# A gated linear attention block followed by a leaky-ReLU MLP on one core: units 0 to 3 as batches of 256 tokens, weights behind unit 0's v, DMA transposes in units 6 to 11, fixed tiles and banks, a new order

## The chip, the cores and the metric

The kernel runs on one core of a Trainium2 chip. The core has five engines, each with a queue of its own that it works through in order: TensorE (PE; PEld is its weight load), VectorE (DVE), ScalarE (ACT), GpSimd (POOL) and SyncE (SP, which here only issues DMAs). Sixteen DMA engines move data between the chip's memory and the core. The metric is the time of one execution in device microseconds.

## The reference

Four batches, eight heads, 768 tokens, 48 columns a head. The first part is a recurrence with a decay per key column; its output, 384 columns a token, goes through a two-layer MLP of width 2048.

```python
f = 1.0 / (1.0 + np.exp(-f_logit))
state = np.zeros((B, H, D, D), dtype=np.float32)
for t in range(S):
    state = f[:, :, t, :, None] * state + np.einsum('bhd,bhe->bhde', k[:, :, t], v[:, :, t])
    y[:, :, t] = np.einsum('bhd,bhde->bhe', q[:, :, t], state)
x = y.transpose(0, 2, 1, 3).reshape(B * S, H * D)
h = x @ w_in
out = np.maximum(0.01 * h, h) @ w_out
```

Inputs and output are float32; the kernel's matmuls are bf16 into float32.

## The kernel before

The recurrence is done in chunks of 128 tokens. With cumulative sums of the log decays, k is scaled up and q scaled down, so that inside a chunk the result is a masked product (q k^T) v, and what came before is q times a state matrix that is carried from chunk to chunk and decayed at its end.

A *unit* is one chunk of two batches: unit j is chunk j // 2 of batches 2(j % 2) and 2(j % 2) + 1, twelve units in all. 128 tokens lie on the 128 partitions, one token to a partition, and the two batches side by side. For a unit, the parts run in this sequence (in brackets the word that stands for each in the order list):

- loads of f, k, q, v by SyncE (`Lf`, `Lk`, `Lq`, `Lv`, line 98), one DMA for each batch of the unit: 128 partitions times 8 heads, 192 bytes a piece. Six buffers for each of the four inputs.
- ScalarE: Exp and Ln of the gate (`gate`, lines 121 and 122).
- TensorE: cumulative sum over tokens as a product with a triangular matrix, and sums over the whole chunk (`cs`, lines 127 and 130).
- ScalarE: three Exp of these (`dec`, lines 137 to 141).
- VectorE or GpSimd: k and q times their factors (`k`, `q`, lines 146 and 152); GpSimd: casts of v (`v`, lines 159 and 160). A cast `v_b` and a zero-padded copy `v2` serve the product with v in strips of 32 columns.
- TensorE: transposes of k and q through an identity matrix, four to a group (`tk`, `tq`, line 173); VectorE copies them out of PSUM (`ck`, `cq`, line 176).
- TensorE: products of k and q (`sc`, called score, line 192); VectorE: the mask (`mk`, line 197).
- TensorE: products with v and with the state (`mx`, mix, line 225); VectorE copies the result out as `xT` (`xt`, line 231).
- state: TensorE (`pt`, line 236), VectorE adds it (`sf`, lines 241 and 242), GpSimd decays and casts it (`sb`, lines 246 and 249).
- MLP: eight `up` (line 256, six matmuls of 256 columns each, a pair of 128-wide blocks of the hidden layer), eight relus on ScalarE (`pr`, line 262), for each of the two batches four quarters of `down` (`dn`, line 267, four matmuls of 384 columns each), VectorE's copy (`ob`, line 272) and the store by SyncE (`st`, line 277).

The weights are loaded by GpSimd with a cast to bf16 (`WI`, line 107, nine DMAs; `WO`, line 111, four). Ahead of each stands a one-element copy (line 103) that waits for the v of a unit: unit 1 for w_in, unit 2 for w_out.

Nothing reorders the work: a list of words in the kernel gives the order in which all instructions are issued, and each engine's queue is this list cut down to its own. The engines run apart from each other as far as data and buffers allow. PSUM has three pools: two banks for `up`, two for `down`, four for everything else.

Of the kernel before, what the change touches and what calls it, by code (L numbers as in the profile page):

```python
# [9 lines left out]
FP32 = mybir.dt.float32  # L10
BF16 = mybir.dt.bfloat16
# [4 lines left out]
def kernel(  # L16
# [21 lines left out]
    pairs = [(c, h) for c in range(NCH) for h in range(B // 2)]  # L38
    NP = len(pairs)
    BY_UNIT = 4  # L40
    K_DVE = 3
    Q_DVE = 2

    const = ctx.enter_context(tc.tile_pool(name="const", bufs=1))
    inp = ctx.enter_context(tc.tile_pool(name="inp", bufs=6))
    work = ctx.enter_context(tc.tile_pool(name="work", bufs=2))
    gpool = ctx.enter_context(tc.tile_pool(name="gpool", bufs=4))
    opool = ctx.enter_context(tc.tile_pool(name="opool", bufs=4))

# [19 lines left out]
    ut = const.tile([128, 128], BF16, tag="ut")  # L69
    make_upper_triangular(nc, ut, val=1.0, diag=True)  # L70
# [3 lines left out]
    nc.gpsimd.memset(ones_col, 1.0)  # L74
    gate_w = const.tile([1, 8], FP32, tag="gate_w")

    w_in_b = const.tile([128, NK, FF], BF16, tag="w_in")
    w_out_b = const.tile([128, NF, KD], BF16, tag="w_out")

    for t in v2s:  # L80
        nc.gpsimd.memset(t[:, :, 1:3, :], 0.0)
    for t in state_b + state_f:
        nc.gpsimd.memset(t, 0.0)

    st = {j: {} for j in range(NP)}
    srcs = {"f": f_logit, "k": k, "q": q, "v": v}

    def once(j, key, make):
        if key not in st[j]:
            st[j][key] = make()  # L90
        return st[j][key]

    def raw(j, name):
        return once(j, name + "_raw", lambda: inp.tile([128, 2, H, D], FP32, name=f"{name}_raw", tag=f"{name}_raw"))

    def load(j, name, a):
        c, h = pairs[j]
        nc.sync.dma_start(out=raw(j, name)[:, a],  # L98
                          in_=srcs[name][2 * h + a, :, c * C:(c + 1) * C, :].rearrange("h t d -> t h d"))

    def weights(which, j):

        nc.gpsimd.tensor_copy(out=gate_w[:, 0:1], in_=raw(j, "v")[0:1, 1, H - 1, D - 1:D])
        if which == "in":
            for lo, hi in ((0, FF // 4), (FF // 4, FF // 2), (FF // 2, FF)):
                for kk in range(NK):
                    nc.gpsimd.dma_start(out=w_in_b[:, kk, lo:hi], in_=moe_w_in[kk * 128:(kk + 1) * 128, lo:hi])
        else:
            n = NF // 4
            for part in range(4):  # L110
                nc.gpsimd.dma_start(  # L111
                    out=w_out_b[:, part * n:(part + 1) * n, :],
                    in_=moe_w_out[part * n * 128:(part + 1) * n * 128, :].rearrange("(a p) n -> p a n", p=128))

    def half(j, i):
        return slice(i, i + 1) if j < BY_UNIT else slice(0, 2)

    def gate(j, i):
        e = work.tile([128, 2, H, D], FP32, name="e_t", tag="e_t")
        a = half(j, i)  # L120
        nc.scalar.activation(e[:, a], raw(j, "f")[:, a], AF.Exp, scale=-1.0)  # L121
        nc.scalar.activation(lfs[j % NR][:, a, :, 0:D], e[:, a], AF.Ln, bias=1.0)  # L122

    def cs(j, a):
        lf = lfs[j % NR]
        t = st[j]["cs", a] = ps_g.tile([128, 512], FP32, name="cs", tag="g")
        nc.tensor.matmul(t[:, 0:H * D], ut, lf[:, a, :, 0:D], start=True, stop=True)  # L127
        if pairs[j][0] < NCH - 1:
            for p in range(P2):
                nc.tensor.matmul(t[:, H * D + p:H * D + p + 1], lf[:, a, 2 * p:2 * p + 2, :], ones_col,  # L130
                                 start=True, stop=True)

    def dec(j, a):
        t = st[j].pop(("cs", a))
        em = once(j, "em", lambda: work.tile([128, 2, H * D], BF16, name="em_t", tag="em_t"))
        at = once(j, "a", lambda: work.tile([128, 2, H * D], BF16, name="a_t", tag="a_t"))
        nc.scalar.activation(em[:, a], t[:, 0:H * D], AF.Exp, scale=1.0)  # L137
        nc.scalar.activation(at[:, a], t[:, 0:H * D], AF.Exp, scale=-1.0)  # L138
        if pairs[j][0] < NCH - 1:
            end = st[j]["end", a] = work.tile([128, P2], FP32, name="a_end", tag="a_end", bufs=8)  # L140
            nc.scalar.activation(end, t[:, H * D:H * D + P2], AF.Exp, scale=-1.0)  # L141

    def scale_k(j, i):
        a = half(j, i)
        eng = nc.vector if j < K_DVE else nc.gpsimd
        eng.tensor_mul(khs[j % NR][:, a, :, 0:D], raw(j, "k")[:, a],  # L146
                       st[j]["em"][:, a].rearrange("t a (h d) -> t a h d", d=D))

    def scale_q(j, i):
        a = half(j, i)  # L150
        eng = nc.vector if j < Q_DVE else nc.gpsimd
        eng.tensor_mul(qhs[j % NR][:, a, :, 0:D], raw(j, "q")[:, a],  # L152
                       st[j]["a"][:, a].rearrange("t a (h d) -> t a h d", d=D))

    def cast_v(j, i):
        a = half(j, i)
        vb = once(j, "v", lambda: work.tile([128, 2, H, D], BF16, name="v_b", tag="v_b", bufs=3))
        v2 = once(j, "v2", lambda: v2s[j % 3])
        nc.gpsimd.tensor_copy(out=vb[:, a], in_=raw(j, "v")[:, a])  # L159
# [21 lines left out]
    def units(a):  # L181
        return range(2) if a == 2 else (a,)
# [199 lines left out]
```

## Time and profile before

| | us |
|---|---|
| median of three runs | 197.61 |
| lowest and highest of them | 197.46, 198.98 |
| span of the profiled execution | 195.7 |
| TensorE busy in the span | 177.3 |
| ScalarE, VectorE, GpSimd busy | 98.4, 93.4, 83.3 |

The profile shows one execution; its own time outside the span is not listed. The span runs from the first to the last instruction. In the profile's rows L256 is line 256 of the kernel; "po<-w_out_b,gT" names what is written and what is read; "SPq" and "POOLq" are the queues' issuing of DMAs. A busy TensorE is not TensorE at its peak, because the ends of matmuls are modelled and overlap.

### The profile page before, as it was taken

The numbers are of one execution on the slowest core, as the hardware profiler recorded it, in microseconds if no ns is written. First come the engines' busy times: TensorE is split into PE (matmuls) and PEld (weight loads), VectorE is DVE, ScalarE is ACT, GpSimd is POOL, SyncE is SP. The second block draws the span as 40 slices with busy tenths as digits, with TensorE's granted clock in tenths as the row PEclk, the third lists the DMA queues.
The fourth block names the chain that finished last, engine by engine and source line by source line (L and its number), as shares of the span: only waits on it lengthen the run. The fifth ranks groups of instructions, "written<-read, shape, count | busy, mean of one in ns | idle before, by whom it ended". The sixth has DMA issues, their size and how long they took to land.

```text
span 195.7 us, 5241 instructions
## 1 busy us (share of the span) xinstructions
PE 177.3 (91%) x2152; PEld 130.7 (67%) x2152; DVE 93.4 (48%) x203; ACT 98.4 (50%) x197; POOL 83.3 (43%) x145
## 2 busy tenths in 40 slices
PE   0686379999999999999979999999999999999993
PEld 0455237777667687787756867777777777777761
DVE  2699614273327438347581149168373146553111
ACT  5645415893234748776155752854324736154430
POOL 8145845928400762795332902984204420500000
PEclk9999999999999999999996999999999999999999
DMA  6999999899999999899999999220001110110112
GB/s 134 216 216 185 166 196 208 162 183 186 190 222 215 222 198 226 159 228 219 200 201 232 183 232 209 44 78 6 18 27 40 45 40 3 40 40 3 40 44 80
DMA packets 106728, 27.08 MB, mean 138 GB/s; under 512 B 100432, under 2 KB 106320, under 8 KB 106704
## 3 DMA queue, kind: packets, MB, share of 16 engines
q1 hardware_dynamic: 103296, 23.60, 57.1%
q0 software_dynamic: 3408, 3.15, 10.1%
q8 instruction: 17, 0.28, 0.6%
q14 instruction: 7, 0.06, 0.1%
HBM read 25.17 MB, written 4.72 MB: 153 GB/s over the span
## 4 chain that ended last, share of the span: by engine, by line
PE 69%; DMA 15%; SPq 11%; POOL 2%; issue 1%; ACT 1%; DVE 1%; POOLq 0%
PE po L267 30%; PE pm L256 25%; SPq L98 10%; DMA q_raw<-in_q_dram 7%; DMA w_out_b<-in_moe_w_out_dram 7%; PE py L225 4%; PE tp L173 4%; PE pw L192 2%; DMA f_raw<-in_f_logit_dram 1%; PE cs L127 1%; POOL w_out_b L111 1%; PE pt L236 1%; SPq L277 1%; POOL qh L152 0%; ACT e_t L121 0%
## 5 line engine op out<-in xcount | busy, mean ns | idle before, releaser
L262 ACT ACTIVATE gT<-pm 128x512 bf16<-128x512 f32 x96 | 57.0, 598 | 75.0 <-PE pm L256 74.5
L256 PE MATMUL pm<-xT,w_in_b 128*128 128x256 bf16 x576 | 79.7, 278 | 5.0 <-DMA w_in_b<-in_moe_w_in_dram 3.6
L267 PE MATMUL po<-w_out_b,gT 128*128 128x384 bf16 x384 | 75.9, 328 | 0.1
L256 PEld LDWEIGHTS <-w_in_b 128*128 128x128 bf16 x576 | 54.8, 99 | 19.1 <-DMA w_in_b<-in_moe_w_in_dram 4.4
L267 PEld LDWEIGHTS <-gT 128*128 128x128 bf16 x384 | 36.2, 98 | 17.2 <-issue 0.6
L197 DVE TENSOR_TENSOR wm<-pw,ut 128x512 bf16<-128x512 f32 x48 | 30.1, 683 | 9.1 <-PE pw L192 9.1
L272 DVE COPY osb<-po 128x384 f32<-128x384 f32 x24 | 13.4, 557 | 40.7 <-PE po L267 40.5
L246 POOL TENSOR_TENSOR sf<-sf,a_end 128x192 f32<-128x192 f32 x20 | 10.7, 535 | 27.1 <-DVE sf L242 26.4
L146 POOL TENSOR_TENSOR kh<-k_raw,em_t 128x768 bf16<-128x768 f32 (+1 forms) x10 | 15.0, 1495 | 15.0 <-ACT em_t L137 8.3
L249 POOL CAST sb<-sf 64x192 bf16<-64x192 f32 x40 | 14.2, 356 | 16.1 <-PE py L225 13.8
L159 POOL CAST v_b<-v_raw 128x384 bf16<-128x384 f32 (+1 forms) x16 | 10.9, 681 | 23.7 <-DMA v_raw<-in_v_dram 15.7
L231 DVE CAST xT<-py 128x384 bf16<-128x384 f32 x24 | 12.4, 553 | 15.7 <-PE py L225 15.2
L176 DVE COPY kT<-tp 128x512 bf16<-128x512 bf16 x24 | 9.8, 420 | 20.7 <-PE tp L173 20.7
L152 POOL TENSOR_TENSOR qh<-q_raw,a_t 128x768 bf16<-128x768 f32 (+1 forms) x12 | 16.8, 1399 | 0.5 <-DMA q_raw<-in_q_dram 0.4
L121 ACT ACTIVATE e_t<-f_raw 128x384 f32<-128x384 f32 (+1 forms) x16 | 11.0, 687 | 9.4 <-DMA f_raw<-in_f_logit_dram 9.3
L127 PE MATMUL cs<-lf,ut 128*128 128x384 bf16 x24 | 8.3, 366 | 7.3 <-ACT lf L122 6.6
L137 ACT ACTIVATE em_t<-cs 128x384 bf16<-128x384 f32 x24 | 11.8, 493 | 4.9 <-PE cs L130 4.6
L176 DVE COPY qT<-tp 128x512 bf16<-128x512 bf16 x24 | 9.8, 419 | 5.2 <-PE tp L173 5.0
L138 ACT ACTIVATE a_t<-cs 128x384 bf16<-128x384 f32 x24 | 12.0, 499 | 0.0
L122 ACT ACTIVATE lf<-e_t 128x384 bf16<-128x384 f32 (+1 forms) x16 | 10.9, 683 | 0.5
L173 PE MATMUL tp<-ident,kh 128*128 128x128 bf16 x96 | 9.6, 233 | 1.5 <-ACT a_end L141 1.0
L130 PEld LDWEIGHTS <-lf 128*128 128x128 bf16 x80 | 5.2, 103 | 8.1 <-issue 6.7
(40 smaller groups left out, 139.0 us busy)
## 6 DMA issues: line engine op xcount, KB each, us to landing
f_raw<-in_f_logit_dram SPq DMA_DIRECT2D x24, 192.0 KB, 3.7
k_raw<-in_k_dram SPq DMA_DIRECT2D x24, 192.0 KB, 3.7
q_raw<-in_q_dram SPq DMA_DIRECT2D x24, 192.0 KB, 3.8
v_raw<-in_v_dram SPq DMA_DIRECT2D x24, 192.0 KB, 3.8
out_dram<-osb SPq DMA_DIRECT2D x24, 192.0 KB, 2.0
w_out_b<-in_moe_w_out_dram POOLq DMA_DIRECT2D x4, 384.0 KB, 9.5
w_in_b<-in_moe_w_in_dram POOLq DMA_DIRECT2D x6, 128.0 KB, 6.1
w_in_b<-in_moe_w_in_dram POOLq DMA_DIRECT2D x3, 256.0 KB, 9.2
```

The lines of the kernel that those rows point to most:

```text
L98: nc.sync.dma_start(out=raw(j, name)[:, a], in_=srcs[name][2 * h + a, :, c * C:(c + 1) * C, :].rearrange("h t d -> t h d"))
L146: eng.tensor_mul(khs[j % NR][:, a, :, 0:D], raw(j, "k")[:, a], st[j]["em"][:, a].rearrange("t a (h d) -> t a h d", d=D))
L152: eng.tensor_mul(qhs[j % NR][:, a, :, 0:D], raw(j, "q")[:, a], st[j]["a"][:, a].rearrange("t a (h d) -> t a h d", d=D))
L173: nc.tensor.transpose(tp[:, p, :], scaled(j, x)[:, a, 2 * p:2 * p + 2, :], ident)
L176: nc.vector.tensor_copy(out=turned(j, x)[:, P2 * a:P2 * a + P2, :], in_=st[j].pop(("tp" + x, a)))
L197: nc.vector.tensor_mul(wm, st[j].pop(("pw", a, i)), ut[:, None, :].to_broadcast([128, P2, 128]))
L231: nc.vector.tensor_copy(out=xT[:, :, a, :], in_=st[j].pop(("py", a))[:, 0:NK, :])
L249: nc.gpsimd.tensor_copy(out=sb[rows, a, :, i * D:i * D + D], in_=sf[rows, a])
L256: nc.tensor.matmul(pm[:, i, :], w_in_b[:, kk, ff * 128:(ff + 1) * 128], st[j]["xT"][:, kk].rearrange("t a s -> t (a s)"), start=(kk == 0), ...
L262: nc.scalar.activation(gT[:, 2 * g:2 * g + 2, :], st[j].pop(("pm", g)), AF.Prelu, alpha=0.01)
L267: nc.tensor.matmul(po, st[j]["g"][:, ff, 128 * a:128 * a + 128], w_out_b[:, ff, :], start=(ff == 0), stop=(ff == NF - 1))
L272: nc.vector.tensor_copy(out=osb, in_=st[j].pop(("po", a)))
```

## The change

- **Units 0 to 3** are now batches: unit j holds chunks 0 and 1, that is 256 tokens, of batch j. Two neighbouring tokens lie on one partition, so a piece of a load has 384 bytes, and one DMA (`_2`) brings both halves of the heads; unit 0 is loaded in two halves of four heads. Chunk 0 lies on partitions 0 to 63 and chunk 1 on 64 to 127. The cumulative sum takes four matmuls of 192 columns with two triangular matrices (`bu`, `bs`, with and without the diagonal), the score takes 32 matmuls with 64 rows and 64 columns of the array each, the mix 64 matmuls with 64 rows and 32 columns, and the state part of chunk 1 follows in a step of its own (`ms`). These units are called *paired*.
- **Units 4 to 11** stay as they were: chunks 2 to 5 of two batches.
- **Weights.** The copy that holds w_in back reads unit 0's v (`Hv_0`), the one for w_out unit 2's k (`Hk_2`). w_in comes in three DMAs, w_out in four whose pieces are 6 KB long: partition p of a quarter holds rows 4p to 4p + 3. So that the hidden layer fits this, the weight loads of `up` read every fourth column of w_in.
- **Transposes** of units 6 to 11 are DMA transposes issued by SyncE (`xk`, `xq`) in place of TensorE's transposes and VectorE's copies. In units 0 and 1 six copies go to ScalarE.
- **Buffers.** All tiles are fixed and indexed by the unit's number; PSUM is eight banks, and each word in the list names its banks. `gT` has three buffers instead of four.
- **Set-up** on GpSimd: the masks `bu`, `bs`, `pair_mask`, `half_ones`, and eight `sb` tiles to clear instead of two `sb` and two `sf`.
- **Order.** A new list.

```diff
-    pairs = [(c, h) for c in range(NCH) for h in range(B // 2)]
+    NA = 4
+    units = [(b, None) for b in range(B)] + [(c, h) for c in range(2, NCH) for h in range(B // 2)]
...
+    PIECES = (512, 512, 1024)
+    w_in_b = [const.tile([128, NK, n], BF16, name=f"w_in{i}", tag=f"w_in{i}") for i, n in enumerate(PIECES)]
+    w_out_b = tiles(4, [128, 4, KD], BF16, "w_out")
+
+    def w_in_of(ff, kk):
+        g, jj = divmod(ff, 4)
+        lo = 512 * g
+        for t, n in zip(w_in_b, PIECES):
+            if lo < n:
+                return t[:, kk, lo + jj:lo + 512:4]
+            lo -= n
...
+            if paired(j):
+                h = slice(0, H) if a == 2 else slice(4 * a, 4 * a + 4)
+                nc.sync.dma_start(out=by_pair(raw(j, x))[:, h].rearrange("t h s d -> t h (s d)"),
+                                  in_=srcs[x][j, h, 0:2 * C, :].rearrange("h (t s) d -> t h (s d)", s=2))
...
+    def hold(x):
+        def go(j):
+            nc.gpsimd.tensor_copy(out=gate_w[:, 0:1], in_=raw(j, x)[0:1, 1, H - 1, D - 1:D])
+        return go
+
+    def load_w_in(i):
+        lo = sum(PIECES[:i])
+        nc.gpsimd.dma_start(out=w_in_b[i],
+                            in_=moe_w_in[:, lo:lo + PIECES[i]].rearrange("(k p) n -> p k n", p=128))
+
+    def load_w_out(g):
+        nc.gpsimd.dma_start(out=w_out_b[g],
+                            in_=moe_w_out[512 * g:512 * g + 512, :].rearrange("(p a) n -> p a n", a=4))
...
+        if paired(j):
+            h = slice(4 * a, 4 * a + 4)
+            for s in range(2):
+                o = t[:, 192 * s:192 * s + 192]
+                nc.tensor.matmul(o, bu, lf[:, 0, h, 0:D], start=True, stop=False)
+                nc.tensor.matmul(o, bu if s else bs, lf[:, 1, h, 0:D], start=False, stop=True)
+            for n in range(2):
+                p = 2 * a + n
+                for s in range(2):
+                    nc.tensor.matmul(t[:, 384 + 2 * n:386 + 2 * n], lf[:, s, 2 * p:2 * p + 2, :], half_ones,
+                                     start=(s == 0), stop=(s == 1))
+            return
...
+    def turn_dma(x):
+        def go(j):
+            nc.sync.dma_start_transpose(out=turned(j, x), in_=scaled(j, x).rearrange("t a h d -> t (a h d)"))
+        return go
...
+        if paired(j):
+            q2 = qT.rearrange("t (s p) n -> t p s n", s=2)
+            for s in range(2):
+                for n in range(2):
+                    p = 2 * a + n
+                    for i in range(2):
+                        for y in range(2):
+                            rows, cols = slice(64 * y, 64 * y + D), slice(64 * i, 64 * i + 64)
+                            o = banks[bank[y]][cols].rearrange("t (s p m n) -> t s p m n", s=2, p=2, m=2)
+                            nc.tensor.matmul(o[:, s, n], kT[rows, P2 * s + p, cols], q2[rows, p, :, cols],
+                                             start=True, stop=True)
+            return
...
+    def mix_state(j):
+        q2 = turned(j, "q").rearrange("t (s p) n -> t p s n", s=2)
+        jobs = []
+        for g in range(NQ):
+            p, n = divmod(g, 3)
+            jobs.append((1, g, state_of(j, 1)[:, p, 32 * n:32 * n + 32], q2[:, p, :, 64:128]))
+        accumulate(j, jobs, (1,))
...
+            if paired(j):
+                src = src.rearrange("t (k s n) -> t k s n", k=NK, s=2)
+                dst = xT[:, :, i, :].rearrange("t k (n s) -> t k s n", s=2)
```

The beginning of the new list, to the first `down`, and two later stretches of which the prediction speaks. A number behind @ is a bank; a last digit 1 in `k`, `q` stands for GpSimd, in `ck`, `cq` for ScalarE.

```
Lf_0_0 Lf_0_1 Lk_0_0 Lq_0_0 Lv_0_0 ge_0_0 Lk_0_1 gl_0_0 Lq_0_1 ge_0_1 cs_0_0@0 Lv_0_1 gl_0_1 Lf_1_2 cs_0_1@1
dec_0_0 Lk_1_2 k_0_0_0 v_0_0 Lq_1_2 dec_0_1 q_0_0_0 tk_0_0@2 Lv_1_2 k_0_1_0 tq_0_0@3 ck_0_0_1 Lf_2_2 q_0_1_0
tk_0_1@4 cq_0_0_1 Lk_2_2 tq_0_1@5 Hv_0 ck_0_1_1 v_0_1 sc_0_0@6.7 Lq_2_2 cq_0_1_1 Lv_2_2 WI_0 mk_0_0_0
pt_0_2@0.1 ge_1_0 Lf_3_2 mk_0_0_1 ge_1_1 sc_0_1@2.3 WI_1 gl_1_0 sf_0_0 mx_0_0@4.5 gl_1_1 Lk_3_2 mk_0_1_0
WI_2 cs_1_0@6 mk_0_1_1 sb_0_0 cs_1_1@7 dec_1_0 sf_0_1 Lq_3_2 mx_0_1 dec_1_1 q_1_0_1 k_1_0_0 k_1_1_0 ms_0
q_1_1_1 tk_1_0@0 xt_0_0_0 tq_1_0@2 ck_1_0_1 tk_1_1@3 xt_0_1_0 sb_0_1 tq_1_1@6 ck_1_1_1 cq_1_0_0 up_0_0@1
cq_1_1_0 up_0_1@7 pr_0_0 sc_1_1@4.0 pr_0_1 sc_1_0@5.2 mk_1_1_0 mk_1_0_0 up_0_2@3 mk_1_0_1 up_0_3@6 mk_1_1_1
pr_0_2 pr_0_3 Lv_3_2 v_1_0 up_0_4@1 v_1_1 up_0_6@7 Lf_4_0 ge_2_0 pr_0_4 pt_1_2@4.5 pr_0_6 up_0_5@2 sf_1_0
gl_2_0 Lk_4_0 Hk_2 WO_0 ge_2_1 mx_1_2@0.3 pr_0_5 sb_1_0 up_0_7@6 xt_1_0_0 gl_2_1 Lq_4_0 WO_1 sf_1_1 ms_1
pr_0_7 cs_2_0@1 WO_2 xt_1_1_0 cs_2_1@7 dec_2_0 Lv_4_0 sb_1_1 up_1_1@4 k_2_0_0 dec_2_1 up_1_5@2 k_2_1_0 WO_3
tk_2_0@0 pr_1_1 up_1_6@5 v_2_0 ck_2_0_0 pr_1_5 tk_2_1@6 pr_1_6 up_1_2@3 q_2_0_1 ck_2_1_0 dn_0_0_0@1 pr_1_2
...
dec_7_1 up_5_7@2 Lq_10_0 ob_4_0_0 ge_9_2 up_5_0@5 q_7_2_1 st_4_0 pr_5_7 up_5_4@6 pr_5_0 up_5_3@4 gl_9_2
...
pr_8_2 up_8_4@1 pr_8_0 up_8_3@4 pr_8_4 dn_8_0_0@0 pr_8_3 cs_11_0@6 cs_10_0@3 dn_8_1_0@2 dec_11_0 k_11_2_1
mx_9_2@5.7 dec_10_0 dn_8_1_1 xt_9_0_0 q_11_2_1 xt_9_1_0 xk_11 dn_8_0_1 up_9_4@1 up_9_3@4 q_10_2_1 pr_9_4
xq_11 dn_8_1_2 pr_9_3 up_9_6@6 k_10_2_1 xq_10 dn_8_1_3 pr_9_6 up_9_7@3 ob_8_1_0 dn_8_0_2 st_8_1 pr_9_7 xk_10
up_9_5@5 up_9_1@7 pr_9_5 up_9_2@1 pr_9_1 up_9_0@4 pr_9_2 dn_8_0_3 pr_9_0 sc_11_2@6.2.3.5 ob_8_0_0 dn_9_0_0@7
mk_11_0_0 st_8_0 dn_9_1_0@1 mk_11_1_1 dn_9_0_1 mk_11_0_1 mk_11_1_0 sc_10_2@4.0.6.5 dn_9_0_2 mk_10_0_0
```

572 lines of the change are left out of this document (342 added, 230 removed).

## The prediction

> **What bounds the kernel now.** I read the page first, then the chain of waits, then the timeline of the first 53 us.
>
> ```profile
> PE 177.3 (91%) x2152; PEld 130.7 (67%) x2152; DVE 93.4 (48%) x203; ACT 98.4 (50%) x197; POOL 83.3 (43%) x145
> ...
> PE   0686379999999999999979999999999999999993
> ...
> DMA  6999999899999999899999999220001110110112
> ```
>
> TensorE is full from about slice 7 on, with one dip in slice 21. The DMA engines are full from the start to slice 25 (about 125 us). So there are two limits side by side: the matmul stream, and the loads that feed it. The chain of waits (start, length, what) gives the prices:
>
> ```profile
> 7.33 0.68 SPq L98
> ...
> 21.10 0.70 SPq L98
> ...
> 38.38 12.87 DMA w_out_b<-in_moe_w_out_dram
> ...
> 52.97 5.20 PE po L267 x32
> ...
> 61.57 0.55 PE pw L192 x16
> 62.13 0.76 PE pm L256 x6
> 62.89 0.65 PE po L267 x4
> ...
> 65.36 0.90 PE py L225 x56
> ...
> 72.03 0.66 PE pm L256 x6
> ...
> 97.84 2.78 DMA f_raw<-in_f_logit_dram
> 100.65 0.85 ACT e_t L121
> ...
> 102.90 1.23 PE pm L256 x6
> ...
> 138.62 0.89 PE tp L173 x16
> ...
> 192.32 0.56 DVE osb L272
> ```
>
> In the full stretch one `up` (6 matmuls) costs 0.655, one quarter of `down` 0.65, a `score` 0.55 and 0.10 more in the group behind it (0.76 against 0.66), a `mix` 0.90 and the same 0.10, four transposes 0.222. The timeline gives a `cs` (0.27, from 42.88 to 43.15) and a `state` (0.17, to 43.32):
>
> ```profile
> 42.88 0.33 PE L127 MATMUL cs<-lf,ut 128*128 128x384 bf16 x1
> ...
> 43.15 0.33 PE L236 MATMUL pt<-v_b,kh 128*128 128x96 bf16 x4
> ...
> 43.32 0.81 PE L267 MATMUL po<-w_out_b,gT 128*128 128x384 bf16 x4
> ```
>
> Counting the order list at these prices: 96 `up` 62.9, 96 quarters 62.4, `score` 7.8 (ten full, four half), `mix` 11.1 (ten at 1.0, four first-chunk halves at 0.275), 48 transpose groups 10.7, `cs` 20 x 0.27 + 4 x 0.17 = 6.1, `state` 20 x 0.17 = 3.4. Sum 164.4. The last matmul ended at 192.3, when the final copy began, so **27.9 us of TensorE time were lost**. The list ahead of the row at 52.97 (20 `up`, 8 quarters, 4 half and 1 full `score`, the same of `mix`, 14 transpose groups, 8 `cs`, 6 `state`) is worth 28.6, so 24.4 of the 27.9 were lost before 53 us, and 3.5 after. Nearly all of the 3.5 is one event: the second half of unit 9's f is issued at 97.84, ScalarE stands at its Exp until 100.65, the relus behind it are late, and TensorE goes on at 102.90 with a slow group. Behind the last matmul the span has 3.4 us, and the median of the runs is 1.9 above the span of 195.7; the profiled execution's own time is not listed apart, so I carry this 1.9 as what lies around a span.
>
> **The change: the matmul stream.** `up` and `down` keep their counts: 125.3. Units 6 to 11 lose 24 transpose groups (DMA does them): -5.3. Paired units: each `cs` half has four 192-column and four 2-column matmuls instead of one 384-column and four: 0.27 + 0.17 = 0.44 by the columns streamed (384 take 0.163 in `down`), 8 of them. Their `score` has 32 matmuls of 64 rows and columns a unit; the nearest rows are 34 ns (0.55/16) and 16 ns (0.90/56) each, 0.51 to 1.10, I take 0.84. `mix` 64 matmuls of 64 rows, 8 to 16 ns, plus 12 for the state: 1.2 a unit (0.8 to 1.3). `state` 16 matmuls, 0.34 to 0.68, take 0.5. Sum: 125.3 + score 8.6 + mix 12.9 + transposes 5.3 + cs 7.4 + state 4.0 = **163.5** (160 to 167): the stream itself hardly changes.
>
> **The strided weights.** Each of the 576 `up` weight loads now reads every fourth column. No weight load before does.
>
> ```profile
> L256 PEld LDWEIGHTS <-w_in_b 128*128 128x128 bf16 x576 | 54.8, 99 | 19.1 <-DMA w_in_b<-in_moe_w_in_dram 4.4 <-issue 2.2
> ```
>
> The 99 ns is a latency: transposes follow each other at 0.89/16 = 55.6 ns, a load each. An `up` matmul takes 109 ns and covers the load. Twice 55.6 is 111: +2 ns x 576 = 1.1 us; four times is 222: +113 x 576 = 65 us. A gain is excluded, since the load is covered already. I take 0, as the cover is twofold. The Trainium skill (TensorE: Matmul & The Clock Gate, "Weight-path perf modes") says that fast weight load reads 32 bits, two bf16, at a time; with every fourth column that would halve the rate and the sum would be 1.1 us longer. No run here shows it.
>
> **Loads.** The nearest rows for the price of a piece are the loads' queue, a stretch in which only stores run, and the issues with their time to landing:
>
> ```profile
> q1 hardware_dynamic: 103296, 23.60, 57.1%
> ```
>
> ```profile
> 140.00:150.00 10.00, 10.00 (x143) 7.45 (x142) 6.23 (x13) 3.58 (x6) 1.67 (x4) 1.00 0.12 41
> ```
>
> ```profile
> v_raw<-in_v_dram SPq DMA_DIRECT2D x24, 192.0 KB, 3.8
> out_dram<-osb SPq DMA_DIRECT2D x24, 192.0 KB, 2.0
> ...
> w_out_b<-in_moe_w_out_dram POOLq DMA_DIRECT2D x4, 384.0 KB, 9.5
> ...
> w_in_b<-in_moe_w_in_dram POOLq DMA_DIRECT2D x3, 256.0 KB, 9.2
> ```
>
> From 140 to 150 us only stores run: share 0.12 of 16 engines, 410 KB, 267 rows of 1536 B, so 72 ns a row. The queue's 57.1% is 1788 us of engine time; less 3072 stored rows at 72 ns, 98,304 pieces of 192 B cost 15.9 ns each. A line through both gives 23.9 ns for the 384 B pieces of units 0 to 3 (bounds: 15.9, no cost by size; 31.8, no gain). 32,768 pieces become 16,384: 521 us become 392, and 129/16 = **8.1 us of DMA time go** (0 to 16.3), all in the first third.
>
> **The start.** Before the change w_in waits for unit 1's v and w_out for unit 2's (timeline; behind it rows of the groups):
>
> ```profile
> 19.20 0.18 POOL L103 COPY gate_w<-v_raw 1x1 f32<-1x1 f32 x1 [1.73 <-DMA v_raw<-in_v_dram]
> ...
> 24.77 0.53 POOL L107 DMA_DIRECT2D w_in_b<-in_moe_w_in_dram  x1 [0.98 <-DMA w_in_b<-in_moe_w_in_dram]
> 25.27 3.80 SPq L98 DMA_DIRECT2D v_raw<-in_v_dram  x1
> ...
> 26.46 1.03 PE L256 MATMUL pm<-xT,w_in_b 128*128 128x256 bf16 x4 [0.68 <-DMA w_in_b<-in_moe_w_in_dram]
> ...
> 29.12 5.05 SPq L98 DMA_DIRECT2D f_raw<-in_f_logit_dram  x1
> ...
> 35.98 0.18 POOL L103 COPY gate_w<-v_raw 1x1 f32<-1x1 f32 x1
> ```
>
> ```profile
> L176 DVE COPY kT<-tp 128x512 bf16<-128x512 bf16 x24 | 9.8, 420 | 20.7 <-PE tp L173 20.7
> ...
> L152 POOL TENSOR_TENSOR qh<-q_raw,a_t 128x768 bf16<-128x768 f32 x8 | 13.1, 1642 | 0.0
> ...
> L159 POOL CAST v_b<-v_raw 128x384 bf16<-128x384 f32 x8 | 4.3, 538 | 7.0 <-DMA v_raw<-in_v_dram 4.0 <-ACT a_t L138 3.0
> ...
> L83 POOL MEMSET sb<- 128x768 bf16 x2 | 1.4, 740 | 0.0
> L81 POOL MEMSET v<- 128x256 bf16 x3 | 0.8, 311 | 0.0
> ```
>
> After the change unit 0's v is the gate, the eighth load: issued by 8.0 with the old pieces, landed 3.8 later at 11.8, about 9.5 with the new ones. But GpSimd has its own list first: eight `sb` memsets of half the size (0.37 each, 3.0), 25 small set-up operations (0.31 at most, I take 0.2: 5.0) from 0.7, so 8.7, then both halves of `v` (0.54 and about 0.55 for the small copies, each) and the gate: w_in is issued at about **11.1** (to 13). Unit 0's state casts and unit 1's scaling of q stand behind this gate on GpSimd; they are wanted after unit 0's masks, later than 13. From the gate to the last matmul operand of the first w_in third took 26.46 - 19.20 = 7.3; to the last third 24.77 + 9.2 - 19.20 = 14.8. So the first `up` runs at 18.4 (its place in the list, worth 6.2: lost 12.2) and the fifth, at 9.6 in the list, at 24.5 to 25.9: lost 15 to 16. The gain is thinner further on. k of unit 2, the gate of w_out after the change, is load 20 counted in 192 KB. Before, 22 loads went out by 21.80, 0.96 each; with the new pieces 0.72, so 14 by 11. While w_in moves they take 4 to 5 us each (rows at 25.27 and 29.12), three quarters of that with the new pieces: 4 more by 25, the last two by 27. The last quarter of w_out landed at 38.38 + 12.87 = 51.25, 15.3 behind its gate at 35.98, so now it lands at 42; the list wants it at 24.9, that is 40 with 15.5 lost. The same gate holds up unit 1's state casts on GpSimd, which the state part of its `mix` wants at 13.6 in the list (29.1): 27 + 0.2 + 0.5 for the issue + 0.6 for two casts, 28.3. I take **17 lost by then** (13 to 22) against 24.4.
>
> **Later.** Fixed banks let eight `up` run at a row where two banks did; before, TensorE lost only 0.6 apart from the event at 100, so I take no gain for that. The event: after the change unit 9's Exp stands at 78.9 in the list, wanted at 78.9 + 17 = 95.9; its data come at 100.65 - 8.1 and about 1 for one transpose in front of it, 93.5. Just in time, so I keep 3.5 for this kind of stall (0 to 8). The copies that move to ScalarE (6 of 0.42) lie beside a stream in which ScalarE is half idle (50% of the span); without that cover they are 2.5 us.
>
> **The DMA transposes.** Twelve, 256 KB each, on SyncE's queue behind a wait for GpSimd's scaling; loads for units three ahead and stores stand behind that wait. Not in the trace: the bounds are 2.0 (a store's landing) and 9.5 (w_out's), I take 3.7, nearest the 192 KB loads. Tightest is the end: unit 11 and 10 have four scalings of 1.64 on GpSimd from 124.9 in the list, done at 131.5, landed at 135.2, wanted at 136.7. Hidden, with 1.5 to spare.
>
> **Sum.** 163.5 + 17 + 3.5 = 184.0 for the last matmul, + 3.4 = 187.4 of span, + 1.9 = **189.3 us**, 4.2% under the median of 197.61.
>
> **Rivals.** *Small pieces don't gain.* If a 384 B piece costs two of 192 B, the start loses about 20, and unit 9's f comes at 101.6 against 78.9 + 20 = 98.9: 2.7 of stall, about 1 of slow matmuls, 0.6 elsewhere. 163.5 + 20 + 4.3 + 5.3 = **193.1**. Against it speaks that the rows of 1536 B cost 72 ns, not eight times 15.9 = 127. The Trainium skill (DMA: Bandwidth & Descriptors, "Specifications") says that line rate needs 512 B or more; by that rule 384 B still pays the penalty, and this case would hold.
>
> *Transposes one behind the other, slower than before.* Place: SyncE's queue, units 8 to 11. If they don't overlap and each holds the queue for T, four of them from 126.6 in the list end at 126.6 + 4T + 1 against 136.7: it costs something from T = 2.3, and eats the gain of 8.3 from T = 4.6. At T = 5 the end costs 10.9 and units 8 and 9 (98.6 + 4T + 1 against a score at 115.8) 3.8 more: **204**. For it: one in-order queue and the wait for scaling. Against: loads of 192 KB land in 3.8 while several are in flight.
>
> *Strided weights slower than a matmul covers.* The gain of 8.3 is gone at 109 + 8300/576 = 123 ns a load; at four times 55.6, 189 + 65 = **254**. Against: the cover of 109 ns.
>
> *The change doesn't start w_in earlier* because GpSimd's set-up is longer than I count: 25 x 0.31 puts the gate at 14, 3 us more: 192, inside the first case.
>
> **Numbers.** Forecast 0.57 (180 to 196), no gain by pieces 0.18 (189 to 198), transposes 0.16 (196 to 212), weights 0.09 (above 199). 181.5 to 201 leaves out about 0.03 below and 0.17 above. A measurement of this kernel can tell about 1% from no change (195.6 to 199.6): faster 0.56 + 0.15 = 0.71, same 0.01 + 0.03 + 0.03 = 0.07, slower 0.13 + 0.09 = 0.22.
>
> **What would show it.** The gate's copy at about 11, the first `pm` at about 18, the fifth `up` at 25, the last matmul near 184; `pm` groups still 0.655 in the full stretch (weights); the queue's engine time lower by about 130 us for loads (pieces); the last four transposes landed before the `score` of unit 10 (transposes); no wait of ScalarE for f of unit 9 over 3 us. I am wrong if the start loses more than 22, if `score` waits for a transpose, or if `pm` spacing exceeds 111 ns.

## The result, and the profile after

| | us |
|---|---|
| before, median of 4 runs (lowest, highest) | 197.54 (196.65, 198.98) |
| after, median of 4 runs (lowest, highest) | 186.04 (185.05, 186.86) |
| ratio, with its 95% interval | 0.9412 [0.9341, 0.9484] |
| after again in a later session, 6 runs (before there 197.06, 10 runs) | 184.98, ratio 0.9406 [0.9356, 0.9457] |
| profiled execution after: its own time, its span | 186.37, 184.6 |

Medians here and below are of all runs; the ratios leave out runs more than 1.5% above the fastest of their kernel.

The forecast was 189.3, the range 181.5 to 201. The page of the changed kernel, with the same rows as before the change and that of the granted clock of TensorE, PEclk (a row has 40 slices, here of 4.6 us each; a digit is tenths):

```profile
PE 170.2 (92%) x2304; PEld 132.8 (72%) x2304; DVE 84.0 (46%) x173; ACT 100.9 (55%) x203; POOL 82.6 (45%) x164
...
PE   0896659999999999999999999999999999999992
...
PEclk9999978999999999999999999999999999999999
DMA  5999999999999999989996989995110671110022
GB/s 134 303 311 197 210 291 248 218 197 178 209 243 183 231 205 236 203 180 241 171 217 151 230 165 195 231 138 123 65 67 4 114 156 46 46 43 0 4 85 85
...
q1 hardware_dynamic: 99392, 26.75, 64.5%
```

TensorE is full from slice 7 to the end, without the dip in the middle that the kernel before had in slice 21. The 16 DMA engines are still full to slice 27 (about 125 us), nearly as before (25, 122 us). The loss is now all in the first third, and the timeline of that part shows where (start, length, engine, line, what, and in brackets the idle time ahead with its releaser):

```profile
9.71 0.18 POOL L156 COPY gate_w<-v_raw 1x1 f32<-1x1 f32 x1
...
10.63 2.48 POOL L161 DMA_DIRECT2D w_in<-in_moe_w_in_dram  x3
...
17.87 1.47 PE L457 MATMUL ps<-xT,w_in 128*128 128x256 bf16 x12 [0.46 <-DVE xT L413]
...
20.32 1.50 PE L457 MATMUL ps<-xT,w_in 128*128 128x256 bf16 x12 [0.41 <-DMA w_in<-in_moe_w_in_dram]
...
25.32 2.60 PE L457 MATMUL ps<-xT,w_in 128*128 128x256 bf16 x12 [3.51 <-DMA w_in<-in_moe_w_in_dram]
...
25.62 0.18 POOL L156 COPY gate_w<-k_raw 1x1 f32<-1x1 f32 x1 [6.00 <-DMA k_raw<-in_k_dram]
```

The first `up` runs at 17.87 (26.46 before) and waits for `xT`, not for a weight. The fifth waits 3.51 for the half of w_in that comes in one DMA. The chain of waits says what lies behind that:

```profile
5.51 2.87 POOL sb L115 x8
...
10.69 1.45 POOL w_in L161 x2
...
12.35 12.93 DMA w_in<-in_moe_w_in_dram
25.32 2.60 PE ps L457 x12
...
29.60 0.74 PE ps L351 x61
...
36.93 0.45 PE ps L424 x16
...
39.26 0.57 PE ps L313 x32
39.83 0.78 PE ps L457 x6
...
53.34 0.27 PE ps L221
...
181.24 0.56 DVE osb L480
```

It goes back from the fifth `up` over w_in's last DMA to GpSimd's set-up. From 53.34 on (the first `cs` of unit 4) everything in it up to the final copy is TensorE's own work, and the windows view agrees (us of the stretch, busy time with matmuls, granted clock, DMA share, GB/s):

```profile
53.34:181.24 127.90, 127.81 (x1605) 1.00 0.65 138
```

One loss is no wait. Two `up` take 2.60 at 25.32, where two take 1.31 later. The granted clock is the reason: 0.50 to 0.59 from 25.32 to 28.67 and 0.84 to 29.60, then 1.00 (slices 6 and 7 of PEclk), which makes this stretch an estimated 1.7 us longer than at the full clock (the missing part of the clock, summed over 25.32 to 29.60). In e11, the same kernel in another session, the drop lies at 18.04 (two `up` in 2.75), ahead of a wait for w_in, and the first `cs` of unit 4 comes at 51.63. A wait alone doesn't bring it: in e3 two `up` take 1.50 right after a wait of 3.01. What sets it off is not shown.

### The profile page after: what moved, and what is told of

Same layout as the page of the kernel before. It is cut to its first block, busy times and chain, and to the rows that moved or that the text cites. A ratio compares the mean times of both kernels' runs of the same rounds, so it can differ in the third digit from the quotient of the medians.

```text
span 184.6 us, 5590 instructions
## 1 busy us (share of the span) xinstructions
PE 170.2 (92%) x2304; PEld 132.8 (72%) x2304; DVE 84.0 (46%) x173; ACT 100.9 (55%) x203; POOL 82.6 (45%) x164
## 4 chain that ended last, share of the span: by engine, by line
PE 82%; DMA 7%; POOL 6%; DVE 2%; issue 1%; ACT 0%; POOLq 0%; DVEq 0%
PE ps L457 34%; PE ps L469 34%; DMA w_in<-in_moe_w_in_dram 7%; PE ps L351 5%; PE ps L320 2%; PE ps L277 2%; POOL sb L115 2%; PE ps L221 1%; PE ps L429 1%; POOL pair_mask L110 1%; POOL w_in L161 1%; PE ps L313 1%; PE ps L424 1%; DVE wm L330 1%; DVE osb L480 1%
## 5 line engine op out<-in xcount | busy, mean ns | idle before, releaser
L462 ACT ACTIVATE gT<-ps 128x512 bf16<-128x512 f32 x96 | 56.6, 603 | 51.8 <-PE ps L457 39.5
L457 PE MATMUL ps<-xT,w_in 128*128 128x256 bf16 x576 | 69.9, 276 | 4.4 <-DMA w_in<-in_moe_w_in_dram 3.9
L469 PE MATMUL ps<-w_out,gT 128*128 128x384 bf16 x384 | 71.4, 326 | 0.0
L457 PEld LDWEIGHTS <-w_in 128*128 128x128 bf16 x576 | 62.5, 115 | 8.0 <-DMA w_in<-in_moe_w_in_dram 4.8
L480 DVE COPY osb<-ps 128x384 f32<-128x384 f32 x24 | 13.3, 554 | 43.5 <-PE ps L469 29.4
L232 ACT ACTIVATE em<-ps 128x384 bf16<-128x384 f32 x24 | 11.8, 493 | 18.8 <-PE ps L224 14.8
L334 DVE TENSOR_TENSOR wm<-ps,ut 128x512 bf16<-128x512 f32 x32 | 20.0, 682 | 3.8 <-PE ps L320 3.7
L244 POOL TENSOR_TENSOR qh<-q_raw,at 128x768 bf16<-128x768 f32 (+1 forms) x14 | 18.8, 1353 | 4.4 <-issue 4.1
L449 POOL CAST sb<-sf 64x192 bf16<-64x192 f32 x40 | 13.9, 348 | 12.7 <-PE ps L351 5.5
L413 DVE CAST xT<-ps 128x384 bf16<-128x384 f32 x24 | 12.7, 564 | 13.5 <-PE ps L351 13.4
L244 POOL TENSOR_TENSOR kh<-k_raw,em 128x768 bf16<-128x768 f32 x8 | 13.2, 1651 | 11.9 <-ACT em L232 11.6
```

The source lines that it names most:

```text
L232: nc.scalar.activation(ems[j % 2][:, a], t[:, 0:H * D], AF.Exp, scale=1.0)
L244: eng.tensor_mul(heads(j, to[j % NR], a)[:, :, :, 0:D], raw_heads(j, x, a), decays(j, by, a))
L334: nc.vector.tensor_mul(w, src.rearrange("t (p n) -> t p n", p=P2), ut[:, None, :].to_broadcast([128, P2, 128]))
L413: nc.vector.tensor_copy(out=dst, in_=src)
L449: nc.gpsimd.tensor_copy(out=sb[rows, :, y * D:y * D + D], in_=sf[rows])
L457: nc.tensor.matmul(pm[:, i, :], w_in_of(ff, kk), xTs[j % 3][:, kk].rearrange("t a s -> t (a s)"), start=(kk == 0), stop=(kk == NK - 1))
```

## The experiments

Every ratio is to the kernel before, run in the same session; the medians of before were 196.75 (e1 to e4), 196.65 (e5 to e8) and 197.06 (e10 to e12).

| run | us | ratio |
|---|---|---|
| e1, w_in held by unit 1's v | 190.98 | 0.9688 [0.9612, 0.9763] |
| e2, paired loads in 192 B pieces, two DMAs each | 195.46 | 0.9911 [0.9862, 0.9961] |
| e3, transposes of units 6 to 11 on TensorE | 193.32 | 0.9822 [0.9753, 0.9891] |
| e4, neighbouring columns in the weight loads | 186.10 | 0.9464 [0.9374, 0.9555] |
| e5, paired loads in 384 B pieces, two DMAs each | 190.41 | 0.9675 [0.9613, 0.9736] |
| e6, set-up behind w_in's issue | 185.27 | 0.9406 [0.9350, 0.9462] |
| e7, the same and w_in in four pieces | 184.84 | 0.9310 [0.9240, 0.9380] |
| e12, e7 again | 185.88 | 0.9439 [0.9392, 0.9486] |
| e10, the same and unit 10's f earlier | 186.00 | 0.9426 [0.9368, 0.9484] |
| e8, kernel *before* with w_in held by unit 0's v | 200.19 | 1.0185 [1.0132, 1.0238] |

**e1: w_in one unit later.**

```diff
-    ... tq_0_1@5 Hv_0 ck_0_1_1 v_0_1 ... Lv_2_2 WI_0 mk_0_0_0
-    ... sc_0_1@2.3 WI_1 gl_1_0 ... mk_0_1_0
-    WI_2 cs_1_0@6 ... q_1_1_1 tk_1_0@0
+    ... tq_0_1@5 ck_0_1_1 v_0_1 ... Lv_2_2 mk_0_0_0
+    ... sc_0_1@2.3 gl_1_0 ... mk_0_1_0
+    cs_1_0@6 ... q_1_1_1 Hv_1 WI_0 WI_1 WI_2 tk_1_0@0
```

> The changed kernel, but w_in waits for unit 1's v as before the change, its issue standing behind unit 1's scaling of q on GpSimd. Everything else is as in the changed kernel (186.04 us, w_in issued at 10.6, fifth up at 25.3). Theory A (the earlier start of w_in is the larger part of the gain): issue at about 16.5, fifth up at 29 to 32, and since the rest of the order follows it, 189 to 193 us. Theory B (the gain is the shorter load time of units 0 to 3): the loads of units 1 and 2 come earlier by what w_in no longer takes, w_out is issued earlier, and the time stays within 1.5 of 186.

It took 190.98 us, 4.9 more than the changed kernel. The profiled execution was the slowest of its runs (193.75), so only rows from its first 33 us are used:

```profile
16.45 0.18 POOL L156 COPY gate_w<-v_raw 1x1 f32<-1x1 f32 x1
16.58 2.49 POOL L161 DMA_DIRECT2D w_in<-in_moe_w_in_dram  x3
...
24.04 2.75 PE L457 MATMUL ps<-xT,w_in 128*128 128x256 bf16 x12 [7.08 <-DMA w_in<-in_moe_w_in_dram]
...
32.71 2.15 PE L457 MATMUL ps<-xT,w_in 128*128 128x256 bf16 x12 [2.42 <-DMA w_in<-in_moe_w_in_dram]
```

w_in is issued 6.0 later, the first `up` runs 6.2 later and the fifth 7.4, of which 4.9 reach the end. So the place of the hold is a part of the gain in the new list.

**e8: the same move in the kernel before.**

```diff
-    ... v_0_1 mk_0_0_0 ... q_1_1 WI_1 ck_1_0
+    ... v_0_1 WI_0 mk_0_0_0 ... q_1_1 ck_1_0
```

> The kernel before, with the hold of w_in on unit 0's v instead of unit 1's; nothing else. Theory A, an earlier w_in alone is worth little: the list puts the first up behind two units' products, and 192-byte loads of units 1 and 2 fall back by what w_in takes: 195 to 200 us against 196.75, first up no earlier than 25. Rival B, the place of the hold is the gain by itself: 190 to 193 us, as moving it back cost the changed kernel 4.9 us.

200.19 us, 3.5 slower. The chain of waits:

```profile
13.78 14.24 DMA q_raw<-in_q_dram
...
30.78 0.70 DVE wm L197
...
32.10 1.40 PE pm L256 x6
```

Unit 1's second q, issued at 13.78 while w_in moves (its nine DMAs are issued from 11.99 on), takes 14.24 to land; before, the same load, issued at 13.73, took 3.6. In the old list the first `up` stands behind unit 1's products, so it runs at 32.1 instead of 26.5. Rival B falls: the place of the hold is not the gain by itself. The change also has a list that asks for unit 0's `up` before unit 1's score, and loads of larger pieces; which of these makes the early w_in pay was not tried apart.

**e2 and e5: the pieces and the number of DMAs.** e2 splits each paired load by token parity (192 B pieces), e5 by heads (384 B pieces); both have twice the DMAs.

```diff
 # e2
-                nc.sync.dma_start(out=by_pair(raw(j, x))[:, h].rearrange("t h s d -> t h (s d)"),
-                                  in_=srcs[x][j, h, 0:2 * C, :].rearrange("h (t s) d -> t h (s d)", s=2))
+                for s in range(2):
+                    nc.sync.dma_start(out=by_pair(raw(j, x))[:, h, s],
+                                      in_=srcs[x][j, h, 0:2 * C, :].rearrange("h (t s) d -> t h s d", s=2)[:, :, s])
 # e5
+                mid = (h.start + h.stop) // 2
+                for h in (slice(h.start, mid), slice(mid, h.stop)):
+                    nc.sync.dma_start(out=by_pair(raw(j, x))[:, h].rearrange("t h s d -> t h (s d)"),
+                                      in_=srcs[x][j, h, 0:2 * C, :].rearrange("h (t s) d -> t h (s d)", s=2))
```

> The changed kernel, but each load of units 0 to 3 is split into two DMAs by the token's parity, so that its pieces have 192 bytes again; layout, order and everything else unchanged. Theory A (a 384 B piece costs about 24 ns against 2 x 15.9): the loads' queue gets 16384 more pieces and some 130 us more engine time, unit 2's k and unit 9's f come 4 to 8 us later, and ScalarE or TensorE waits for data: 188 to 194 us. Rival (pieces under 512 B gain nothing by being larger): engine time of the queue rises by less than 30 us and the time stays within 1 of 186.

> The changed kernel with every load of the paired units split into two DMAs by heads; the pieces stay at 384 bytes, the number of DMAs is that of the run with 192-byte pieces (195.46 us). Theory A, the size of the pieces is what cost 9.4 us there: 185 to 188 us, the load queue within 60 us of engine time of the changed kernel's 1905, no wait of TensorE for q's scaling over 2 us. Rival B, it was the number of DMAs (20 more issues of 0.5 to 1.1 us on SyncE ahead of unit 3): 190 to 196 us, with the same packets as the changed kernel.

e2 took 195.46, more than its expectation's 188 to 194; e5 took 190.41. So of e2's 9.4 us about half comes from twice the DMAs and half from the small pieces: 4.4 and 5.0 by these medians, 5.2 and 4.6 by the ratios. The runs stand in different sessions, and the changed kernel itself moved by 1.1 between two, so no more than about half each can be read from them. In e5 the time is the one expected by theory B (the number of DMAs), and the engine time the one expected by theory A (51 us more than after, below). The page of e2, then of e5 (DMA queue's row: packets, MB, share of 16 engines):

```profile
GB/s 102 172 199 169 198 209 215 166 198 214 188 188 231 203 203 213 234 217 199 246 173 164 234 200 199 165 250 156 92 44 41 58 202 45 44 41 0 3 81 81
...
q1 hardware_dynamic: 116096, 26.75, 67.3%
```

```profile
GB/s 112 194 244 192 211 243 244 227 211 164 176 213 245 199 212 187 230 154 228 206 205 174 239 203 201 226 220 129 42 45 42 96 171 45 45 42 0 3 83 83
...
q1 hardware_dynamic: 99712, 26.75, 64.5%
```

Spans were 193.9 and 189.5. Engine time of the queue: after 0.645 x 184.6 x 16 = 1905 us, e5 0.645 x 189.5 x 16 = 1956, e2 0.673 x 193.9 x 16 = 2088. Against e5, with the same number of DMAs, e2 has 16,384 pieces more and 132 us more. What the number of DMAs costs is seen in SyncE's timeline of e5:

```profile
0.74 1.99 SPq L148 DMA_DIRECT2D f_raw<-in_f_logit_dram  x4
2.77 0.98 SPq L148 DMA_DIRECT2D k_raw<-in_k_dram  x2
```

Here SyncE takes 0.5 to issue one DMA. Unit 0's quarters carry 96 KB, so the queue gets at most 96 KB in 0.5 us, 197 GB/s, and the second slice moved 194. In the changed kernel a DMA carries 192 KB, and the slice moved 303. In e2 one consequence is a wait of TensorE of 9.2 us for unit 1's scaled q, whose load took 13.14; another is that f of units 9 and 10 came late again, the kind of stall that the kernel before had at 98 to 103. The first is the larger: unit 4's first `cs` runs 7.6 later than in the changed kernel (60.98), the last matmul 9.1 later (190.31), so 1.5 are lost behind it. In e5 these are 3.2 and 4.6 (chain of waits of e2):

```profile
13.63 13.14 DMA q_raw<-in_q_dram
...
26.94 0.92 POOL qh L245
...
100.81 4.41 DMA f_raw<-in_f_logit_dram
...
110.33 5.65 DMA f_raw<-in_f_logit_dram
```

**e3: transposes back on TensorE.** The twelve `xk`, `xq` are replaced by `tk`, `tq` and VectorE's copies, placed ahead of the scores that need them:

```diff
-    dec_7_0 xk_6 ... xq_6 sb_5_1 sc_5_2@3.5.7.0 ... cs_8_0@2 mk_5_1_1
+    dec_7_0 ... sb_5_1 sc_5_2@3.5.7.0 ... cs_8_0@2 tk_6_0@1 ck_6_0_0 tk_6_1@4 ck_6_1_0 mk_5_1_1
...
```

> The changed kernel, but units 6 to 11 transpose on TensorE with VectorE's copies, as before the change, each pair of groups placed 2 to 4 us of matmul work behind the place of the DMA transpose; no DMA transposes. Theory A (TensorE is the limit from 53 us on): 24 groups of 0.222 come into the stream, 5.3 us, with 0 to 1.5 us for waits on copies and banks: 191 to 193 us. Rival (the stream has slack, or SyncE's waits for the transposes cost as much): within 1.5 of 186.

193.32 us, 7.3 more than the changed kernel and a little over the 191 to 193 of theory A. From unit 4's first `cs` (51.97) to the end of the last matmul it takes 135.5, where the changed kernel takes 127.9: 5.3 for the 24 groups of 0.222 that were expected, and 2.3 more, with VectorE's copies now in the chain of waits:

```profile
94.39 0.42 DVE qT L292
94.81 0.94 DVE xT L413 x2
...
122.41 1.02 DVE xT L413 x2
...
156.03 0.44 DVE qT L292
...
187.49 0.56 DVE osb L480
```

The page of e3 also separates the loads from the transposes, since only loads and stores are left on the queue:

```profile
DMA  5999999999999989898999633011110011110022
...
q1 hardware_dynamic: 86720, 23.60, 53.1%
```

0.531 x 191.1 x 16 = 1624 us, against 1788 in the kernel before: 164 less. And the twelve DMA transposes of the changed kernel account for the rest of its 1905: 281 us of engine time, 17.6 us of all sixteen engines. The changed kernel's packet records, summed by size, agree: 285 us in packets of 256 B, which only the transposes make, 23.3 ns for a packet of 384 B and 15.5 for one of 192 B.

**e4: the strided weight loads.**

```diff
-                return t[:, kk, lo + jj:lo + 512:4]
+                return t[:, kk, lo + 128 * jj:lo + 128 * jj + 128]
```

> The changed kernel, but up reads 128 neighbouring columns of w_in for each weight load in place of every fourth; w_out stays as it is, so that hidden columns meet other rows of w_out and the output is another one, while the work is the same in size. Theory A (the matmul of 109 ns covers the strided load): the recorded weight load falls from 115 to about 99 ns, the spacing of up stays at 0.655 for six matmuls, and the time stays within 1 of 186. Rival (strided loads cost TensorE time): 1 to 5 us faster.

186.10 against 186.04. The group of the weight loads, first after, then e4 (busy, mean ns, idle before):

```profile
L457 PEld LDWEIGHTS <-w_in 128*128 128x128 bf16 x576 | 62.5, 115 | 8.0 <-DMA w_in<-in_moe_w_in_dram 4.8
```

```profile
L457 PEld LDWEIGHTS <-w_in 128*128 128x128 bf16 x576 | 55.9, 99 | 14.1 <-DMA w_in<-in_moe_w_in_dram 4.7 <-issue 0.3
```

Every fourth column makes a load 16 ns longer in the records, and two `up` still take 1.31 in both chains of waits. The cover was enough.

**e6, e7, e12, e10: can the start be shortened further?** e6 moves GpSimd's clearing of `sb`, two of three `v2` and the triangular mask behind w_in's issue. e7 and e12 also bring w_in in four equal pieces, and ask for unit 0's `up` in their order. e10 also loads unit 10's second half of f ahead of its k, q and v.

```diff
 # e6
-    for t in v2s:
-        nc.gpsimd.memset(t[:, :, 1:3, :], 0.0)
-    for b in range(B):
-        for t in sbs[b]:
-            nc.gpsimd.memset(t, 0.0)
...
-    make_upper_triangular(nc, ut, val=1.0, diag=True)
+    nc.gpsimd.memset(v2s[0][:, :, 1:3, :], 0.0)
...
+    def clear(n):
+        for t in sbs[n] + (sbs[3] if n == 2 else []):
+            nc.gpsimd.memset(t, 0.0)
+        if n > 0:
+            nc.gpsimd.memset(v2s[n][:, :, 1:3, :], 0.0)
+        if n == 2:
+            make_upper_triangular(nc, ut, val=1.0, diag=True)
...
+    ... WI_2 Z_0 cs_1_0@6 ... sb_0_1 Z_1 tq_1_1@6 ... Z_2 Hk_2 WO_0
 # e7, e12
-    PIECES = (512, 512, 1024)
+    PIECES = (512, 512, 512, 512)
...
+    ... WI_2 WI_3 Z_0 ... up_0_4@1 v_1_1 up_0_5@7 ... up_0_6@2
 # e10
-    dec_8_1 Lk_10_0 ... up_5_7@2 Lq_10_0 ... pr_5_4 Lv_10_0 ... pr_5_5 Lf_10_1
+    dec_8_1 Lf_10_1 ... up_5_7@2 Lk_10_0 ... pr_5_4 Lq_10_0 ... pr_5_5 Lv_10_0
```

> The changed kernel with GpSimd's clearing of sb, of two of the three v2 and the triangular mask moved behind the issue of w_in (3.9 us of its 9.7 before the gate). Theory A, the set-up on GpSimd holds w_in back: the gate's copy at 6 to 8 instead of 9.7, w_in issued at 7 to 9 instead of 10.6, first up at 16 to 17.5, 183 to 185.3 us. Rival B, the loads are what holds it (v of unit 0 lands late, or w_in only takes the same bytes per us from the loads of units 1 and 2): within 0.7 of the changed kernel's 186.0.

> As the run before, and w_in in four pieces of 512 columns instead of 512, 512, 1024, with the fifth to seventh up of unit 0 in the order of the pieces. Theory A, the 3.5 us wait at the fifth up is for one DMA that carries half of w_in: 0.5 to 1.3 us faster than with the later set-up alone. Rival B, the last piece lands no earlier and the sixth up waits instead: within 0.5 of it, or up to 0.8 slower by the fourth issue on GpSimd.

> The kernel with later set-up and four pieces of w_in once more, in more rounds. Theory A, set-up and last piece held the start: 182.5 to 184.5 us, 1.5 to 3.5 below the changed kernel. Rival B, the fast profiled execution of the first time was chance: within 1 of the changed kernel.

> The changed kernel as it is, so that the versions of this call stand beside it on the same chip: 185 to 187 us.

> The kernel with later set-up and four pieces of w_in, and the second half of unit 10's f loaded three places earlier on SyncE's queue, ahead of unit 10's k, q and v. In its profile ScalarE waited 1.7 us for that load at 103.4, behind a DMA of 4.75 us. Theory A, the wait is on the path: 0.7 to 2 us faster than without, 181 to 184 us. Rival B, k and q that now come later are as late, or other work covers it: within 0.6.

None of them is told apart from the changed kernel: 185.27, 184.84, 185.88 and 186.00 against 186.04 and 184.98. e7 looked better when first measured, with four runs between 182.77 and 186.50, but not again as e12, which is the same kernel; so its first value is not a gain. e6 shows why so little comes of the set-up (timeline of GpSimd):

```profile
8.88 0.18 POOL L159 COPY gate_w<-v_raw 1x1 f32<-1x1 f32 x1 [1.01 <-DMA v_raw<-in_v_dram]
...
9.81 2.48 POOL L164 DMA_DIRECT2D w_in<-in_moe_w_in_dram  x3
```

With 3.9 us less to do, GpSimd waits for unit 0's v, and w_in goes out 0.8 earlier: set-up and load end almost together in the changed kernel. In e12's trace no wait for w_in is left, and the `cs` of unit 3 starts at 40.91, where the changed kernel has 43.89 in its first trace and 42.18 in e11. But the traces of one beginning differ as much: e7, the same kernel as e12, has 39.80, and e10, which begins like both, 44.17. In e12 ScalarE then stands for f, and TensorE with it (timeline of ScalarE, then windows of TensorE, both of e12):

```profile
95.20 0.85 ACT L195 ACTIVATE e<-f_raw 128x768 f32<-128x768 f32 x1 [1.43 <-DMA f_raw<-in_f_logit_dram]
...
106.14 0.84 ACT L195 ACTIVATE e<-f_raw 128x768 f32<-128x768 f32 x1 [2.08 <-DMA f_raw<-in_f_logit_dram]
```

```profile
95.00:113.00 18.00, 16.39 (x211) 1.00 1.05 209
```

1.6 us of TensorE are lost there, with the DMA engines full. In e11, the changed kernel in the same session, the Exp of units 9 and 10 run at 94.66 and 103.73 with no wait. It is the loads that differ: the second half of unit 9's f is issued at 90.82 in e12, at 88.23 in e11 and at 88.62 in e7, where the Exp of unit 9 runs at 92.49 without a wait. So what is won at the start can be lost again at units 9 and 10, in one execution and not in another of the same kernel; why its loads come 2 us later is open. e10 takes away these waits, but in its profile TensorE waits 2.2 for w_out at 34 instead; whether that is its own doing or the variation of a run, one profile doesn't tell, and the time is the same.

## Why the prediction was right

The direction, the mechanism and most terms held; the time came out 3.3 us under the forecast. By terms, the start took 0.7 more than forecast, the stalls behind it 3.4 less and the frame 0.1 less, which gives 186.5 against the 186.37 of the profiled execution.

- **Matmul stream, 163.5.** Right. The list ahead of unit 4's first `cs`, counted at the prediction's prices, is worth 35.6, so 127.8 are behind it; TensorE took 127.9 for them. (`mix` adds up to 8 x 1.0 + 4 x 1.2 = 12.8, not 12.9; nothing hangs on it.) Of the paired units' prices, read off the chain of waits above, score was too dear (0.57 and 0.12 in the group behind it, taken 0.84), state a little too cheap (0.45 and 0.12 behind it, taken 0.5), mix right within 0.1 (0.74, 0.13 behind it, and some 0.28 for the state part, taken 1.2).
- **Start, 17 lost.** Right in size, 53.34 - 35.6 = 17.7, but by luck in its last step. Up to the fifth `up` the account held: 25.32 less its place in the list, 9.5, is 15.8 (said 15 to 16). The rest, to 17, was to be a wait for w_out's last quarter, landing at 42 and wanted at 40. It landed at 41.2 and was used at 42.57; TensorE waited for no part of w_out. In its place came the lower clock behind the fifth `up`, an estimated 1.7 us, which is no term of the sum; in e11, where it falls elsewhere, 51.63 - 35.6 = 16.0 are lost. Single steps: gate copy 9.71 (said 11), w_in issued 10.63 (11.1), first `up` 17.87 (18.4), fifth 25.32 (24.5 to 25.9), w_out's gate 25.62 (27). The set-up ended at 8.9 (8.7); the casts of a half of v took 0.8 and not 1.1, and the hold's copy stands between the two halves.
- **Later, 3.5.** This is the term that was mis-sized: it measured 0.1. The prediction had computed unit 9's f as arriving in time (93.5 against 95.9), and kept 3.5 all the same for this kind of stall. (About half of the 3.5 in the kernel before was not the wait but the granted clock behind it: 0.60 and 0.50 from 102.90 to 105.50, 0.65 to 107.00, an estimated 1.7.) Both computed times came close: the load was issued at 89.98 and landed 3.3 later, at 93.3, and the Exp ran at 96.38 without a wait, a margin of 3.1. At unit 10 the margin is 0.7 (landed at 104.8, Exp at 105.44), and e2, with slower loads, and e12 do have such stalls: 1.5 and 2.2 us of TensorE are lost there behind unit 4's first `cs`. The kind of stall is real; here it belonged into the range and not into the sum.
- **Pieces.** A price of 23.9 ns for 384 B was estimated, and loads cheaper by 129 us of engine time; e3 gives 164 us, that is 22.0 ns ((1624 - 3072 x 0.072 - 65,536 x 0.0159) / 16,384), and the packet records 23.3. The rival in which small pieces don't gain would cost 3.8 us over the forecast; e2 against e5 measured 5.0. The Trainium skill (DMA: Bandwidth & Descriptors, "Specifications") puts line rate at 512 B or more; the runs agree that 192 B is worse than 384 B, and add that below that line 384 B is far from the price of two halves (23.3 ns against 31.0). No run here has loads on this queue above 384 B a piece. In the second and third slice 303 and 311 GB/s were moved, where the page of the kernel before has 216 and 216:

```profile
GB/s 134 216 216 185 166 196 208 162 183 186 190 222 215 222 198 226 159 228 219 200 201 232 183 232 209 44 78 6 18 27 40 45 40 3 40 40 3 40 44 80
```

- **What the prediction left out of the loads' account.** "The queue's engine time lower by about 130 us for loads" was to show the pieces, and for loads alone e3 bears it out. The queue's time as a whole rose, from 1788 to 1905 us, because the twelve DMA transposes put 281 us on the same engines, more than the pieces gave back. They run from about 88 us on, where the DMA engines would else be free earlier (e3's row falls after slice 22, at 105 us, the changed kernel's after slice 27, at 125). It cost nothing here, since no wait resulted, but it goes with a narrower margin: in e3, without the transposes, unit 10's f lands 4.5 us before its Exp, in the changed kernel 0.7.
- **DMA transposes.** Landing was taken as 3.7; in the last two rows of the issues (KB each where listed, median us to landing) it is 3.5 and 3.9. They did not hold each other up: the last four are issued 1.5 to 2 us apart, as GpSimd's scalings end, and each lands in 3.1. No score waited; the last of them landed 3.0 ahead of the `score` of unit 10 (1.5 forecast):

```profile
v_raw<-in_v_dram SPq DMA_DIRECT2D x18, 192.0 KB, 4.0
...
v_raw<-in_v_dram SPq DMA_DIRECT2D x3, 384.0 KB, 13.9
...
kT<-kh SPq DMA_TRANSPOSE x6, 3.5
qT<-qh SPq DMA_TRANSPOSE x6, 3.9
```

  The value of the removed groups, 5.3, was right for TensorE alone; undoing the step costs 7.3, with VectorE's copies on the path. That was no term of the sum.
- **Strided weights, 0.** Right (e4). The Trainium skill (TensorE: Matmul & The Clock Gate, "Weight-path perf modes") has fast weight load read 32 bits, two bf16, at a time. What the prediction drew from that, half the rate, would have made it 1.1 longer; the load did get longer, 115 against 99 ns, but it stays under the price of a matmul and no time comes of it.
- **Tail and frame.** 181.2 to 184.6 is 3.4, as taken; the execution's own time is 1.8 above its span (taken 1.9).

Undoing single parts costs 4.9 (hold), 9.4 or 5.0 (pieces with and without twice the DMAs) and 7.3 (transposes). Their sum is more than the 11.5 us gained: they are not to be added, since each is measured with the others in place. The paired layout by itself, and fixed banks and order by themselves, weren't tried.

## What to carry to other kernels

Where two limits lie side by side, price a change against both: a step that moves work from TensorE to the DMA engines is free only as long as the loads keep their lead, and the lead is the number to work out. Before a weight load is moved forward, look whether the list asks for it there and whether the loads behind it can afford it; the same move was worth 4.9 us in one kernel and cost 3.5 in the other. A stall that the arithmetic says will not happen should be put into the range and not kept in the sum as a fixed term. A term that comes out right is not yet a right account: look in the trace for the wait that it stands for.

## What the runs showed of the hardware besides

- A DMA transpose of [128 x 1024] bf16 from SyncE makes some 1,056 packets (12,672 for twelve) and takes 23 us of engine time, 1.5 us of all sixteen engines, though it lands in 3.5 to 3.9.
- SyncE issued the first DMAs of e5 in about 0.5 us each (single ones elsewhere in 0.39); with 96 KB a DMA the load rate there was 194 GB/s (96 KB in 0.5 us are 197), where 192 KB reached 303.
- w_in's transfer slows the loads beside it by several times: the same load, q of unit 1, took 14.24 us to land in e8 and 3.6 before. In the changed kernel the 384 KB loads issued before 9 us landed in 4.3 to 5.2, those issued between 11 and 14, behind w_in's issue at 10.63, in 13.9 to 14.4.
- A weight load that reads every fourth column is recorded 16 ns longer (115 against 99), with no effect on 128x256 matmuls.
- After a wait of 3.51 in the changed kernel and 3.92 in e5, two `up` took 2.60 and 2.75 at a granted clock of about half, which lasted some 3 us; after one of 3.01 in e3 they took 1.50. In e11 the drop follows a wait of only 0.75. In e2 two `up` took 2.56 behind a wait of 9.15, with a recorded clock of 1.00: the record doesn't always show it.
